# Linear attention and an MLP on one core: the first batch's k and v over all 128 partitions, its products in array quarters

## The chip, the core and the metric

The kernel runs on one core of a Trainium2 chip. Its engines work side by side, each through its own queue in order: TensorE (PE) multiplies matrices into PSUM, VectorE (DVE) and ScalarE (ACT) compute on SBUF and PSUM, GpSimd (POOL) computes and issues DMAs, SyncE (SP) issues DMAs. The metric is the device time of one execution in microseconds; the shown times are the median of several runs.

## The reference

Eight batches of eight heads, 576 tokens, 64 values to a head, float32 in and out. Linear attention, then a layer norm and an MLP with a residual:

```python
q_s = exp(q - max) / sum over d          # softmax of each token's q
k_s = exp(k - max) / sum over tokens     # softmax of each column of k
kv  = einsum('bhsd,bhse->bhde', k_s, v)  # 64 x 64 for each head
x   = einsum('bhsd,bhde->bhse', q_s, kv) # -> [B, S, 512]
xn  = (x - mean) / sqrt(var + 1e-6) * g_ln
out = x + relu(xn @ w_ch1) @ w_ch2       # 512 -> 2048 -> 512
```

## The kernel before, in words

The work is cut into nine chunks: chunk b of 0 to 7 is the first 512 tokens of batch b, four tokens to a partition, and chunk 8 gathers the last 64 tokens of all batches. For each chunk the attention gives x, x is centred, transposed so that the model dimension lies on the partitions (`xnT`), multiplied by w1 (2048 columns, `ph` or `bx`, `bb`, `bc`), passed through relu to `hT`, and multiplied by w2. From chunk 1 on both MLP products go by a scheme of seven block products instead of eight. The whole program has its order written out by hand: `run` (L820), under `tc.manual_schedule` (L1071), interleaves a list of MLP products with side work that has a place in units of PE time. Each engine's queue is the order of these calls.

The change touches the prologue, `first_batch` (L938), which makes the first two of chunk 0's four token groups ready for the MLP:

- SP issues the loads of q's tokens 0 and 1 (L951) and then of k in four pieces of two heads (L961). Batch 0's k and v hold all 576 tokens, six to a partition on 96 partitions (`T0`, `P0`, L56).
- DVE clears and fills constants (L968 to L982), among them `kv_sb[:, 1:B]`, whose off-diagonal blocks must be zero for the later batches.
- POOL makes the identity, then copies four columns of q into `gate` (L985). That copy waits for q's landing, and everything behind it in POOL's queue waits with it: the loads of v in three pieces with a cast to bf16 (L987), of q's tokens 2 and 3 (L951), of w1 (L994, L99) and w2 (L103).
- PE runs products on a tile of zeros (`warm`, L838). ACT takes exp of q (L209), DVE sums and normalises it (L218, L264, L904), PE transposes it (`eq_pT`, L909).
- ACT takes exp of k for two heads at a time (`exp_k0`, L283). PE sums it over the tokens by products with a column of ones (`z0_mm`, L296): six products for each pair of heads. `recip_z` (L304) inverts the sums.
- `kv0_mm` (L311): six products of exp(k) with v for a pair of heads, 96 rows by 128 columns each. Only the two 64x64 diagonal blocks of the result are wanted. DVE multiplies by the reciprocal and by a block-diagonal mask `diag` in one instruction and sums each row (L312). ACT (for the last pair DVE) spreads the row sum, times -1/512, over 128 columns, `mbc` (L317, L321).
- `xT_mm` (L332) multiplies `kv_sb` and `mbc` by the transposed exp(q), which gives x centred and transposed straight away in `pxT`; `xT_out` (L341, L343) scales it by g into `xnT`. In between stand exp and transposes of q's tokens 2 and 3.

Then the MLP of chunk 0 begins (`mm1_part`, L505). Its first 16 products need w1's first 512 columns, which come in two pieces (L994). `kv_pairs` (L361) is the later batches' k'v, in two column halves of the array, and `po_mm` (L395) is chunk 8's x, in all four quarters.

Of the kernel before, what the change touches and what calls it, by code (L numbers as in the profile page):

```python
# [12 lines left out]
FP32 = mybir.dt.float32  # L13
BF16 = mybir.dt.bfloat16
AF = mybir.ActivationFunctionType
ALU = mybir.AluOpType
# [4 lines left out]
def kernel(  # L21
# [16 lines left out]
    nc = tc.nc  # L38

    B, H, S, D = q.shape  # L40
    DM = H * D
    DH = 4 * DM
    P = 128
# [3 lines left out]
    KO1 = DM // P  # L47
    KO2 = DH // P
    NP = H // 2
# [3 lines left out]
    C9 = B  # L53
    FAST = 1
    CAST = (1, 2, 3)
    T0 = 6  # L56
    P0 = S // T0
    assert SR == 64 and B % 2 == 0

    const = ctx.enter_context(tc.tile_pool(name="const", bufs=1))  # L60
    wts = ctx.enter_context(tc.tile_pool(name="wts", bufs=1))
    raw = ctx.enter_context(tc.tile_pool(name="raw", bufs=2))
    att = ctx.enter_context(tc.tile_pool(name="att", bufs=2))
    sml = ctx.enter_context(tc.tile_pool(name="sml", bufs=8))
    mlp = ctx.enter_context(tc.tile_pool(name="mlp", bufs=2))
# [3 lines left out]
    att_ps = ctx.enter_context(tc.tile_pool(name="att_ps", bufs=2, space=PS))  # L69
    mm_ps = ctx.enter_context(tc.tile_pool(name="mm_ps", bufs=6, space=PS))  # L70

    ident = const.tile([P, P], BF16)
    eps_ln = const.tile([P, 1], FP32)
    gate = const.tile([P, 4], FP32)
    ones = const.tile([P, 1], BF16)
    junk = const.tile([P, 256], BF16)
    scrap = const.tile([P, 512], BF16)
    bones = const.tile([P, 2], BF16)
    ones_w = const.tile([P, P], BF16)
    diag = const.tile([P, P], FP32)  # L80
    mbc = const.tile([P, NP, P], BF16)
    g_one = const.tile([P, KO1], FP32)
    w1_sb = wts.tile([P, KO1, DH], BF16, name="w1_raw")
    w1g = const.tile([P, KO1, DH], BF16)
# [1 line left out]
    ident_f = const.tile([KO1, KO1], FP32)  # L86
    w2_sb = const.tile([P, KO2, DM], BF16)
    w2_q = const.tile([P, 4, KH, DH2], BF16)
    kv_sb = const.tile([P, B, NP, P], BF16)
    ekr = const.tile([P, 2, H // 2, D], BF16)  # L90
    vr = const.tile([P, 2, H, VW], BF16)
    vm = const.tile([P, 2, T, H, VW], BF16)

    w1_src = moe_w_ch1.rearrange("(ko ki) n -> ki ko n", ki=P)
    w2_src = moe_w_ch2.rearrange("(ko ki) n -> ki ko n", ki=P)

# [11 lines left out]
    raws = {}  # L108
# [66 lines left out]
    eks, eqs, eqTs, xs, xnTs, rstds, tqs = {}, {}, {}, {}, {}, {}, {}  # L175
# [101 lines left out]
    kvbox = {}  # L277

    def exp_k0(j):
        hs = slice(2 * j, 2 * j + 2)  # L280
        if j == 0:
            eks[0] = raw.tile([P, T0, H, D], BF16, tag="kt", name="ek0", bufs=1)
        nc.scalar.activation(  # L283
            eks[0][0:P0, :, hs, :].rearrange("p t h d -> p h t d"), raws[0][0][0:P0, hs], AF.Exp
        )

    def k0_mm(j, t):
        hs = slice(2 * j, 2 * j + 2)
        return eks[0][0:P0, t, hs, :], raws["v0"][0:P0, hs, t, :], P

    def z0_mm(j):

        if j == 0:
            kvbox["z0"] = mm_ps.tile([P, NP], FP32, tag="m", name="z0")
        for t in range(T0):
            nc.tensor.matmul(  # L296
                kvbox["z0"][:, j : j + 1], k0_mm(j, t)[0], ones[0:P0],
                start=(j == 0 and t == 0), stop=(t == T0 - 1), skip_group_check=True,
            )

    def recip_z():
        kvbox["rz"] = sml.tile([P, NP], FP32, tag="rzk", name="rzk")
        kvbox["sum"] = sml.tile([P, NP], FP32, tag="lnv", name="kvs")
        nc.vector.reciprocal(kvbox["rz"], kvbox["z0"])  # L304

    def kv0_mm(j):
        pool, tag = (att_ps, "a") if j < 2 else (mm_ps, "m")
        pkv = pool.tile([P, P], FP32, tag=tag, name="pkv")
        for t in range(T0):
            lhsT, rhs, w = k0_mm(j, t)  # L310
            nc.tensor.matmul(pkv[:, 0:w], lhsT, rhs, start=(t == 0), stop=(t == T0 - 1))  # L311
        nc.vector.scalar_tensor_tensor(  # L312
            kv_sb[:, 0, j, :], in0=pkv, scalar=kvbox["rz"][:, j : j + 1], in1=diag,
            op0=ALU.mult, op1=ALU.mult, accum_out=kvbox["sum"][:, j : j + 1],
        )
        if j < NP - 1:
            nc.scalar.activation(  # L317
                mbc[:, j], ones_w, AF.Copy, scale=kvbox["sum"][:, j : j + 1]
            )
        else:  # L320
            nc.vector.tensor_scalar_mul(  # L321
                out=mbc[:, j], in0=ones_w, scalar1=kvbox["sum"][:, j : j + 1]
            )

    def xT_mm(j, kh):

        if j == 0:
            pobox["T", kh] = mm_ps.tile([P, 2, 2, P], FP32, tag="m", name="pxT")
        ops = [(kv_sb[:, 0, j, :], j % 2)] if j // 2 == kh else []
        ops += [(mbc[:, j], i) for i in range(2)]  # L330
        for n, (lhsT, i) in enumerate(ops):
            nc.tensor.matmul(  # L332
                pobox["T", kh][:, i], lhsT, eqTs[0][:, 0:2, j, :],
                start=(j == 0 and n == 0), stop=(j == NP - 1 and n >= len(ops) - 2),
                skip_group_check=True,
            )

    def xT_out(i):
# [2 lines left out]
            nc.vector.tensor_scalar_mul(out=dst, in0=src, scalar1=g_one[:, i : i + 1])  # L341
        else:
            nc.scalar.activation(dst, src, AF.Copy, scale=g_one[:, i : i + 1])  # L343

    halves = (slice(0, 64), slice(64, P))

    def kv_pairs(b, ts=range(T + 1)):

# [589 lines left out]
    def first_batch():  # L938

        nc.scalar.preload_act_table_set("natural_log_exp_and_others")  # L940
        raws[0] = (
            mlp.tile([P, H, T0, D], FP32, tag="hT", name="kt0", bufs=1), None,
            raw.tile([P, H, T, D], FP32, tag="qt", name="qt"),
        )
        k0, _, q0 = raws[0]
        v0 = mlp.tile([P, H, T0, D], BF16, tag="hs", name="v0", bufs=1)
        raws["v0"] = v0

        def load_q0(t, tn, eng):
            ts = slice(t, t + tn)  # L950
            eng.dma_start(  # L951
                q0[:, :, ts],
                q[0, :, 0:SM, :].rearrange("h (p t) d -> p h t d", t=T)[:, :, ts],
            )

        def src0(x, h0, hn):
            return x[0, h0 : h0 + hn].rearrange("h (p t) d -> p h (t d)", t=T0)

        load_q0(0, 2, nc.sync)
        for h0 in range(0, H, 2):  # L960
            nc.sync.dma_start(  # L961
                k0[0:P0, h0 : h0 + 2].rearrange("p h t d -> p h (t d)"), src0(k, h0, 2)
            )
        raws["g"] = outp.tile([KO1, P], FP32, tag="ot", name="g_rows")
        nc.scalar.dma_start(
            raws["g"], bass.AP(moe_g_ln.tensor, moe_g_ln.offset, [[P, KO1], [1, P]])
        )
        nc.vector.memset(junk, 0.0)  # L968
        nc.vector.memset(eps_ln, 1e-6)
        nc.vector.memset(ones, 1.0)  # L970
        nc.vector.memset(bones, 0.0)
        nc.vector.memset(bones[0:64, 0:1], 1.0)
        nc.vector.memset(bones[64:P, 1:2], 1.0)
        nc.vector.memset(ones_w, -1.0 / DM)
        nc.vector.memset(diag, 0.0)
        for ps in halves:
            nc.vector.memset(diag[ps, ps], 1.0)
        nc.vector.memset(kv_sb[:, 1:B], 0.0)
        nc.vector.memset(vr, 0.0)
        for half in range(2):  # L980
            nc.vector.memset(vr[64 * half : 64 * half + 64, :, 4 * half : 4 * half + 4, D:], 1.0)
        nc.vector.memset(vm[:, :, :, :, D:], 1.0)  # L982
        make_identity(nc, ident)
        nc.gpsimd.tensor_copy(out=ident_f, in_=ident[0:KO1, 0:KO1])
        nc.gpsimd.tensor_copy(out=gate, in_=q0[:, 1, 0, 0:4])  # L985
        for h0, hn in ((0, 4), (4, 2), (6, 2)):
            nc.gpsimd.dma_start(  # L987
                v0[0:P0, h0 : h0 + hn].rearrange("p h t d -> p h (t d)"), src0(v, h0, hn)
            )
        for t in range(2, T):  # L990
            load_q0(t, 1, nc.gpsimd)
        for kh in range(2):
            ks = slice(2 * kh, 2 * kh + 2)
            nc.gpsimd.dma_start(w1_sb[:, ks, 0:512], w1_src[:, ks, 0:512])  # L994
        for nb in range(1, 4):
            load_w1(nb)
        load_w2(0)
        load_w2(1)

        new_eq(0)  # L1000
        start_x(0)
        warm(34)
        for t in range(2):
            exp_qt(0, t)
            norm_q(0, t)
        eq_pT(0, 0, nc.vector)
        warm(11)
        eq_pT(0, 1, nc.vector)
        for j in range(NP):
            exp_k0(j)  # L1010
            z0_mm(j)
            if j == NP - 2:
                g_columns()
        recip_z()
        kv0_mm(0)
        kv0_mm(1)
        kv0_mm(2)
        xT_mm(0, 0)
        kv0_mm(3)
        exp_qt(0, 2)  # L1020
        exp_qt(0, 3)
        xT_mm(1, 0)
        xT_mm(2, 0)
        xT_mm(0, 1)
        xT_mm(3, 0)
        xT_out(0)
        xT_out(1)
        eq_pT(0, 2, nc.scalar)
        xT_mm(1, 1)
        xT_mm(2, 1)  # L1030
        eq_pT(0, 3, nc.vector)
        xT_mm(3, 1)
        xT_out(2)
        xT_out(3)
# [139 lines left out]
```

## Time and profile before

| | us |
|---|---|
| median of 3 runs (264.06, 264.73, 266.44) | 264.73 |
| span of the profiled execution | 262.95 |
| between the two | 1.8 |
| PE busy, idle in the span | 255.6, 7.3 |
| first MLP product (`ph`) starts | 15.04 |
| w1's second piece landed | 16.89 |

The span runs from the first to the last instruction of one profiled execution; the runs' times are those of whole executions, and the difference is what lies around the span. In lines of the timeline the first number is the start in us, the second how long, then engine, line, operation, output and inputs, count, and in brackets the idle time before and what ended it. Lines of groups give busy us, mean ns of one, and idle time. PEld is the loading of the stationary operand, which overlaps PE.

The granted TensorE clock is 0.998 over the span.

### The profile page before, as it was taken

The page shows a single profiled execution, that of the slowest core. Times are in us where ns is not written, and L with a number is a line of the kernel's source. Part 1 is how long each engine was busy: PE and PEld are TensorE (multiplying, and loading weights), DVE is VectorE, ACT ScalarE, POOL GpSimd, SP SyncE. Part 2 cuts the span into 40 slices and gives each one's busy share as a digit, 9 for nine tenths or more (in the row PEclk, how much of TensorE's full clock was granted, in tenths as well). Part 3 has the DMA queues.
Part 4 walks back from the last instruction along what each step waited for, and adds up shares of the span by engine and source line. Part 5 has one row for each costly group of instructions (what it writes and reads, how often), then busy time and mean ns, then how long its engine had stood idle before and what let it go on. Part 6 is the DMA issues. An engine that isn't in the chain of part 4 may idle for free.

```text
span 262.9 us, 6770 instructions
## 1 busy us (share of the span) xinstructions
PE 255.6 (97%) x2656; PEld 220.1 (84%) x2659; DVE 223.4 (85%) x504; ACT 176.8 (67%) x348; POOL 94.2 (36%) x148
## 2 busy tenths in 40 slices
PE   8999999999999999999999999999999999999993
PEld 6789755788878998899899988988898888888882
DVE  6768996989998999799889988998898979977872
ACT  4647780997976886689578957894789277537400
POOL 4953228414039404930781088009100800030000
PEclk9999999999999999999999999999999999999999
DMA  6999999998999995899489938994905323221014
GB/s 204 252 202 207 358 215 269 282 188 260 187 151 341 232 119 58 266 278 111 100 251 280 140 82 270 261 167 100 271 11 107 113 102 44 42 110 52 0 41 120
DMA packets 82504, 45.00 MB, mean 171 GB/s; under 512 B 58084, under 2 KB 79080, under 8 KB 82472
## 3 DMA queue, kind: packets, MB, share of 16 engines
q0 software_dynamic: 32464, 21.76, 45.3%
q1 hardware_dynamic: 49424, 22.29, 40.1%
q10 hardware_dynamic: 584, 0.53, 0.6%
q8 instruction: 20, 0.33, 0.5%
q14 instruction: 12, 0.10, 0.1%
HBM read 36.70 MB, written 9.44 MB: 175 GB/s over the span
## 4 chain that ended last, share of the span: by engine, by line
PE 89%; DMA 4%; POOL 2%; DVE 2%; issue 1%; ACT 0%; POOLq 0%
PE ba L588 20%; PE bx L733 19%; PE bb L733 10%; PE ph L505 8%; PE be L588 5%; PE bb L588 5%; PE bc L588 5%; PE pc L541 5%; PE bc L733 5%; DMA w_raw<-in_moe_w_ch_dram 3%; PE po L404 2%; PE pkv L361 2%; DMA qt<-in_q_dram 2%; PE ptr L909 1%; POOL v L987 1%; POOL qt L951 1%
## 5 line engine op out<-in xcount | busy, mean ns | idle before, releaser
L588 PEld LDWEIGHTS <-hs 128*128 128x128 bf16 x512 | 49.8, 98 | 5.7
L733 PEld LDWEIGHTS <-w_raw 128*128 128x128 bf16 x480 | 45.5, 98 | 6.4 <-issue 1.2
L259 POOL TENSOR_TENSOR tq<-xnT 128x256 bf16<-128x256 bf16 x26 | 16.7, 662 | 75.3 <-DMA xnT<-xn 48.7
L588 PEld LDWEIGHTS <-hT 128*128 128x128 bf16 x384 | 37.2, 98 | 4.3
L733 PEld LDWEIGHTS <-w1g 128*128 128x128 bf16 x360 | 34.3, 98 | 4.5 <-issue 0.4
L733 PE MATMUL bx<-tq,w_raw 128*128 128x256 bf16 x240 | 31.6, 273 | 0.2 <-ACT s L761 0.2
L588 PE MATMUL ba<-w_q,hs 128*128 128x256 bf16 x256 | 30.8, 273 | 0.0
L757 ACT COPY bc<-bx 128x512 f32<-128x512 f32 x30 | 16.7, 595 | 19.0 <-PE bx L733 19.0
L764 DVE TENSOR_TENSOR bb<-bx,s 128x512 f32<-128x512 f32 x30 | 19.5, 695 | 9.8 <-ACT s L761 7.0
L605 POOL DMA_DIRECT2D out_dram<-ot x28 | 15.4, 557 | 23.7 <-DVE ot L599 23.6
L775 ACT ACTIVATE hT<-bb 128x512 bf16<-128x512 f32 x30 | 16.3, 595 | 10.8 <-PE bb L733 9.6
L417 ACT ACTIVATE scrap<-x,mv 128x512 bf16<-128x512 bf16 x32 | 23.1, 722 | 0.3
L775 ACT ACTIVATE hT<-bc 128x512 bf16<-128x512 f32 x30 | 16.3, 595 | 9.4 <-PE bc L733 9.4
L572 DVE TENSOR_TENSOR hs<-hT 128x1024 bf16<-128x1024 bf16 x32 | 21.7, 685 | 0.5 <-ACT hT L775 0.5
L404 PE MATMUL po<-kv_sb,eqT 128*128 128x128 bf16 x128 | 22.0, 219 | 0.0
L767 DVE TENSOR_TENSOR hT<-bx,s 128x512 bf16<-128x512 f32 x30 | 19.3, 684 | 3.1 <-PE bx L733 3.1
L449 DVE SCALAR_TENSOR_TENSOR x<-po,rq 128x512 bf16<-128x512 f32 x30 | 20.5, 684 | 0.9 <-PE po L404 0.8
L218 DVE TENSOR_REDUCE zq<-eq 128x16 f32<-128x1024 bf16 (+1 forms) x20 | 20.8, 1051 | 0.6 <-ACT eq L209 0.5
L613 ACT COPY s<-ba 128x512 f32<-128x512 f32 x15 | 8.8, 584 | 14.4 <-PE ba L588 9.8
L775 ACT ACTIVATE hT<-bx 128x512 bf16<-128x512 f32 x30 | 16.5, 604 | 0.9 <-PE bx L733 0.9
L761 ACT COPY s<-bb 128x512 f32<-128x512 f32 x30 | 16.6, 622 | 0.6 <-PE bb L733 0.6
L588 PE MATMUL ba<-w_sb,hT 128*128 128x256 bf16 x128 | 16.6, 272 | 0.0
(155 smaller groups left out, 553.5 us busy)
## 6 DMA issues: line engine op xcount, KB each, us to landing
out_dram<-ot POOLq DMA_DIRECT2D x30, 256.0 KB, 5.8
qt<-in_q_dram SPq DMA_DIRECT2D x5, 1024.0 KB, 6.0
kt<-in_k_dram SPq DMA_DIRECT2D x5, 1024.0 KB, 12.5
qt<-in_q_dram POOLq DMA_DIRECT2D x2, 1024.0 KB, 12.9
kt<-in_k_dram POOLq DMA_DIRECT2D x2, 1024.0 KB, 14.3
vm<-in_v_dram POOLq DMA_DIRECT2D x16, 128.0 KB, 11.5
w_raw<-in_moe_w_ch_dram POOLq DMA_DIRECT2D x3, 512.0 KB, 10.9
w_sb<-in_moe_w_ch_dram POOLq DMA_DIRECT2D x3, 512.0 KB, 16.4
```

The source lines that it names most:

```text
L218: nc.vector.reduce_sum(eqs[c][1][:, ts], eqs[c][0][:, ts], axis=AX.X)
L259: eng.tensor_tensor(out=dst[:, t], in0=x[:, t], in1=y[:, t], op=ALU.subtract)
L404: nc.tensor.matmul(pobox["p"][:, i * P : i * P + P], eqTs[c][:, t, i, :], kv_sb[:, c, i, :], start=True, stop=True,)
L417: nc.scalar.activation(scrap, x[:, t], AF.Square, bias=mv[:, t, 0:1], scale=-float(DM), accum_out=mv[:, t, 1:2],)
L449: nc.vector.scalar_tensor_tensor(x[:, t].rearrange("p (h d) -> p h d", h=H), in0=pobox[c, t].rearrange("p (h d) -> p h d", h=H), scalar=1. ...
L505: nc.tensor.matmul(ph[:, m % 2, at : at + tn], (w1g if c else w1_sb)[:, ko, m * P : (m + 1) * P], xnTs[c][:, t0 : t0 + tn, ko, :], start=( ...
L572: nc.vector.tensor_tensor(out=dst, in0=x, in1=y, op=op)
L588: nc.tensor.matmul(hbox[bank][:, t], lhsT, rhs, start=first and (own or t == 0) and k == 0, stop=k == KH - 1, skip_group_check=True)
L733: nc.tensor.matmul(dst[:, q], lhsT, rhs, start=first and q == 0 and ko == 0, stop=ko == 1, skip_group_check=True)
L764: nc.vector.tensor_tensor(out=at[g, "b"], in0=at[g, "x"], in1=at[g, "s"], op=ALU.add)
L767: nc.vector.tensor_tensor(out=h_out(g, 1, 1), in0=at[g, "x"], in1=at[g, "s"], op=ALU.add)
L775: nc.scalar.activation(h_out(g, odd, half), at[g, name], AF.Relu)
```

## The change

Batch 0's k and v lie nine tokens to a partition, 64 partitions to a head, two heads above each other on the 128 partitions. A pair of heads is one piece, contiguous in HBM: k comes in four DMAs of 128 x 576 as before on SP, v in three on POOL. Each of `z0_mm` and `kv0_mm` now makes nine products for the upper and nine for the lower head, alternating, on rows and columns 0 to 63 and 64 to 127 of the array: 72 products of 64x64 for each of the two steps, where there were 24 of 96x128. Their results lie in two PSUM tiles each. The reciprocal becomes two of 64 partitions. Of k'v, DVE scales and sums the upper block and ACT the lower one; the mask goes, and batch 0's `kv_sb` is cleared ahead. The mean column is one value to a partition (`kvm`, on DVE), and PE reads it 128 times with step 0.

On POOL the copy into `gate` goes, and the clearing of `kv_sb[:, 1:B]`, 3584 bf16 on each partition, comes from DVE to POOL, ahead of the loads of v. On DVE two constants go (`ones_w`, `diag`), and `ones_f` and `kv_sb[:, 0]` come.

```diff
-    T0 = 6
-    P0 = S // T0
+    T0 = 9
...
     def z0_mm(j):
         if j == 0:
-            kvbox["z0"] = mm_ps.tile([P, NP], FP32, tag="m", name="z0")
+            kvbox["z0"] = [mm_ps.tile([P, NP], FP32, tag="m", name="z0") for _ in halves]
         for t in range(T0):
-            nc.tensor.matmul(
-                kvbox["z0"][:, j : j + 1], k0_mm(j, t)[0], ones[0:P0],
-                start=(j == 0 and t == 0), stop=(t == T0 - 1), skip_group_check=True,
-            )
+            for z0, ps in zip(kvbox["z0"], halves):
+                nc.tensor.matmul(
+                    z0[ps, j : j + 1], eks[0][ps, j, t], ones[ps],
+                    start=(j == 0 and t == 0), stop=(t == T0 - 1), skip_group_check=True,
+                )
...
     def kv0_mm(j):
-        pool, tag = (att_ps, "a") if j < 2 else (mm_ps, "m")
-        pkv = pool.tile([P, P], FP32, tag=tag, name="pkv")
+        pkv = [
+            pool.tile([P, D], FP32, tag=tag, name="pkv")
+            for pool, tag in ((att_ps, "a"), (mm_ps, "m"))
+        ]
         for t in range(T0):
-            lhsT, rhs, w = k0_mm(j, t)
-            nc.tensor.matmul(pkv[:, 0:w], lhsT, rhs, start=(t == 0), stop=(t == T0 - 1))
+            for pk, ps in zip(pkv, halves):
+                nc.tensor.matmul(
+                    pk[ps], eks[0][ps, j, t], raws["v0"][ps, j, t],
+                    start=(t == 0), stop=(t == T0 - 1),
+                )
...
         nc.vector.scalar_tensor_tensor(
-            kv_sb[:, 0, j, :], in0=pkv, scalar=kvbox["rz"][:, j : j + 1], in1=diag,
-            op0=ALU.mult, op1=ALU.mult, accum_out=kvbox["sum"][:, j : j + 1],
-        )
-        if j < NP - 1:
-            nc.scalar.activation(
-                mbc[:, j], ones_w, AF.Copy, scale=kvbox["sum"][:, j : j + 1]
-            )
-        else:
-            nc.vector.tensor_scalar_mul(
-                out=mbc[:, j], in0=ones_w, scalar1=kvbox["sum"][:, j : j + 1]
-            )
+            kv_sb[lo, 0, j, lo], in0=pkv[0][lo], scalar=rz[lo], in1=ones_f[lo],
+            op0=ALU.mult, op1=ALU.mult, accum_out=total[lo],
+        )
+        nc.scalar.activation(
+            kv_sb[hi, 0, j, hi], pkv[1][hi], AF.Copy, scale=rz[hi], accum_out=total[hi]
+        )
+        nc.vector.tensor_scalar_mul(out=kvm[:, j : j + 1], in0=total, scalar1=-1.0 / DM)
...
-        ops += [(mbc[:, j], i) for i in range(2)]
+        ops += [(kvm[:, j : j + 1].to_broadcast([P, P]), i) for i in range(2)]
...
-        nc.vector.memset(kv_sb[:, 1:B], 0.0)
+        nc.vector.memset(ones_f, 1.0)
+        nc.vector.memset(kv_sb[:, 0], 0.0)
+        make_identity(nc, ident)
+        nc.gpsimd.tensor_copy(out=ident_f, in_=ident[0:KO1, 0:KO1])
+        nc.gpsimd.memset(kv_sb[:, 1:B], 0.0)
+        for j0, jn in ((0, 2), (2, 1), (3, 1)):
+            nc.gpsimd.dma_start(
+                v0[:, j0 : j0 + jn].rearrange("p j t d -> p j (t d)"), src0(v, j0, jn)
+            )
...
-        nc.gpsimd.tensor_copy(out=gate, in_=q0[:, 1, 0, 0:4])
-        for h0, hn in ((0, 4), (4, 2), (6, 2)):
-            nc.gpsimd.dma_start(
-                v0[0:P0, h0 : h0 + hn].rearrange("p h t d -> p h (t d)"), src0(v, h0, hn)
-            )
```

## The prediction

> **What bounds the kernel now.** I read the page first, then the chain of waits of the first 30 us, then the timeline of the first 20 us, and last the rows nearest to what the change adds.
>
> ```profile
> PE 255.6 (97%) x2656; PEld 220.1 (84%) x2659; DVE 223.4 (85%) x504; ACT 176.8 (67%) x348; POOL 94.2 (36%) x148
> ...
> DMA  6999999998999995899489938994905323221014
> ```
>
> TensorE is busy for 255.6 of 262.9 us. Everything that the change touches lies in the first 17 us, so it can only pay by letting PE reach its unbroken stretch sooner. The DMA digits say that the 16 DMA engines are full from the first slice on.
>
> ```profile
> 0.74 4.03 DMA qt<-in_q_dram
> ...
> 4.82 0.19 POOL gate L985
> 5.00 2.06 POOL v L987 x3
> 7.07 1.84 POOL qt L951 x2
> 8.91 0.64 POOL w_raw L994
> 9.56 7.33 DMA w_raw<-in_moe_w_ch_dram
> ```
>
> The chain runs q, gate, POOL's DMA issues, then 7.33 us until the second piece of w1 lands at 16.89; there PE goes on. It looks as if the gate cost time. It does not by itself. The windows of this stretch show a DMA share of 1.10 to 1.29 in each 2 us from 4 us on (over 1 means two packets in flight), and the trace's packet records show the first v packet at 7.68, 2.7 us after its issue, just when SP's k packets run out (last at 7.93). The same is seen later: stores that POOL issued at 81.66 send nothing before 85.30, when SP's loads of 77.5 to 80.4 run out. So w1 waits for bytes, not for its issue at 9.56.
>
> ```profile
> 8.71 0.40 PE L909 MATMUL ptr<-ident,eq 128*128 128x128 bf16 x4
> 8.95 0.59 PE L296 MATMUL z<-ones,ek 96*128 96x1 bf16 x18
> 9.47 0.38 PE L934 MATMUL gcp<-ident_f,g_rows 4*128 4x4 f32 x2
> 10.32 1.25 PE L311 MATMUL pkv<-v,ek 96*128 96x128 bf16 x18 [0.24 <-DMA v<-in_v_dram]
> 11.71 0.39 PE L332 MATMUL pxT<-eqT,mbc 128*128 128x256 bf16 x2
> 13.39 0.39 PE L332 MATMUL pxT<-eqT,mbc 128*128 128x256 bf16 x2 [0.19 <-DVE mbc L321]
> 15.03 0.33 PEld L505 LDWEIGHTS <-w_raw 128*128 128x128 bf16 x4 [0.21 <-DMA w_raw<-in_moe_w_ch_dram]
> 16.93 0.33 PEld L505 LDWEIGHTS <-w_raw 128*128 128x128 bf16 x4 [0.38 <-DMA w_raw<-in_moe_w_ch_dram]
> ```
>
> This is PE's own path: transposes of exp(q) at 8.71 (they follow q, ACT and DVE, which the change leaves alone), denominators, k'v, x transposed, and the first MLP products at 15.03. At 16.93 w1 is 0.38 us late. So two paths end almost together: PE's own, with 0.38 us to spare, and DMA's.
>
> **The change part by part.**
>
> POOL: the gate goes, but a memset of 3584 bf16 on each partition stands in its place ahead of the v loads.
>
> ```profile
> masks.py:197 POOL MEMSET ident<- 128x128 bf16 x1 | 0.2, 204 | 0.3 <-POOLq L1158 0.3
> L1158 POOL MEMSET const-bfloat16-1.0<- 128x1 bf16 x1 | 0.1, 102 | 0.0
> ```
>
> 127 more elements take 102 ns, 0.80 ns each, so the memset takes 0.10 + 3583 x 0.80 = 3.0 us. It follows the cast that ends at 1.55, so v is issued at about 4.6 against 4.94. The bounds are nothing (v at 1.6) and 2.6 ns an element, POOL's slowest row here (662 ns for 256 in L259), 9.3 us. I take 3.0, since it is the same operation. v's packets can't start before k's are through at about 7.6, so 0.3 us earlier gains nothing; a memset up to about 4.9 us would also cost nothing (a POOL DMA with SP idle sent its first packet 1.1 us after issue, 208.09 to 209.22).
>
> DMA: k and v each go from 768 packets to 512 larger ones. The records show 80 ns for v's packet (1536 B read) and 100 ns for w1's (2048 B read), so 2304 B take about 111: 512 x 111 / 16 = 3.55 us instead of 3.84. k: 28.6 ns for 512 B, 80.6 for 1536, so about 120 ns, 3.83 instead of 3.87. Together 0.3 us, w1's second piece at about 16.6. Bounds: nothing, and 80 ns whatever the size, which would free 2.5 us.
>
> DVE loses 1.55 us of memset at 2.4 to 4.0 and some small ones. Its first real work starts at 5.46, just after ACT's first exp(q) ends at 5.42, so this gains nothing. ACT's four exp(k) shrink from 768 to 576 elements (about 0.65 instead of 0.84 each) and end near 8.9, held by k's landing; PE reaches the last of them later than that. Nothing again.
>
> PE: 24 denominator products become 72, and 24 k'v products become 72, in alternating quarters. The nearest rows are the later batches' k'v in two column halves, and batch 8's products in all four quarters:
>
> ```profile
> 42.07 0.32 PE L361 MATMUL pkv<-vm,ek 128*64 128x65 bf16 x8
> 42.70 0.20 PE L361 MATMUL pkv<-vr,ekr 128*64 128x65 bf16 x2
> ```
> ```profile
> 210.40 0.45 PE L395 MATMUL po<-kv_sb,eqT 64*64 64x64 bf16 x32
> 210.78 0.77 PEld L733 LDWEIGHTS <-w_raw 128*128 128x128 bf16 x8
> ```
>
> 40 products start within 0.64 us: 16 ns each, two tiles side by side. 32 start within 0.45 - 0.19: 8 ns each, four tiles. The new code alternates two tiles, so I take 16 ns. Entering such a mode costs about 0.1 us and so does leaving it (PE was due at 210.31 and started at 210.40; it left at 210.66 and went on at 210.78). The new order switches six times: into z, out and in around the g column product, out at the first x product, in and out around the fourth k'v.
>
> The path then is: z starts at 9.05 (8.95 + 0.1); 54 x 16 ns to 9.92; g products at 10.0; the last 18 from 10.43 (0.31 as now, 0.1 for the switch) to 10.72. k'v follows at once, since v's first part lands at about 10.1: the first ends at 11.2 (10.83 now). The four take 1.15 us instead of 24 x 59 ns = 1.4.
>
> Evictions: two reciprocals (0.18 each) end at 11.25. DVE's half takes about 0.30 (351 ns for 128 elements, 686 for 512); ACT's about 0.38 (469 ns for 256 and 592 for 512) and 0.2 for its accumulator; the mean column, a 128x1 op like L467, 0.14. From 11.26 this ends at 12.04, and the first x product on it starts there, at 11.71 now. DVE's queue is in order, so the next half waits behind the mean column, which waits for ACT; a round takes 0.5 to 0.6 us. k'v 2 also waits for the first att_ps buffer (DVE, 11.56), and k'v 3 for the second (about 12.33). The last mean column is ready near 13.7, where mbc was at 13.34. ACT's last half ends near 13.5, so its exp(q) of token 2, 12.55 to 13.18 now, ends at about 14.15, and the transposes behind it on PE wait 0.2 us. The first MLP product comes at about 15.5 instead of 15.03, the second w1 piece is reached at 16.55 + 0.49 = 17.04, where it has landed.
>
> The mean column read with step 0 has no row. Bounds: nothing (the 16 loads of mbc take 97 ns and hide under 107 ns steps), and about 1 us, if a load without the wide path takes as long per column as the 64-column ones (110 ns, so 220) and half of that hides. I take nothing: the count of columns is the same.
>
> Sum: PE's path is 0.49 later, 0.38 of it was waiting anyway: +0.11 us on the execution's span, 263.05. The span shown is 262.95; 264.73 - 262.95 = 1.8 us lie around it by the median, so **264.8 us**.
>
> **The rivals.**
>
> A, slower: the two quarters do not overlap, and each product costs what a product of today costs, 25 ns for z (18 within 0.59 - 0.16) and 59 for k'v. 48 more of each are 1.2 + 2.8 us, less the 0.3 that I counted (2.30 for all against 2.0 now): +3.7 on the forecast, 268.5. It decides from an average step of 34 ns on ((2.6 us / 144) + 16). The 8 and 16 ns rows speak against it; that none of them alternates just two quarters on the diagonal speaks for it.
>
> B: the quarters overlap, but no product starts less than 25 ns after the one before, today's z step: 144 x 9 ns = 1.3 us, 266.1. Against it stand the 8 and 16 ns rows. The Trainium skill, "TensorE: Matmul & The Clock Gate", section "Wait — 56ns, not 53.3ns?", states this floor, about 25 ns however small the product; by it the time would be 266.1, and the traced 8 and 16 ns disagree.
>
> C: v's packets take turns with k's as soon as they exist, at about 5.7 (4.6 + 1.1). k, with 2.2 us to go, would end up to 2.2 us later, at 10.1; the last exp(k) ends at 10.8 and the last z at 11.1, 0.4 after mine: 265.2. For it: the gate's place. Against it: the stores of 81.66 that did not start beside SP's loads. The Trainium skill, "DMA: Bandwidth & Descriptors", section "Queues, rings and completion order", has each engine go round its queues packet by packet, which speaks against ungating v; by that the time is 265.2, and the 3.6 us wait at 81.66 disagrees.
>
> D, a little faster: the quarters run at 8 ns, 144 x 8 = 1.2 us sooner. Then w1's landing at 16.6 decides: 264.73 - 0.3 = 264.4. More is not to be had, whatever POOL and DVE save.
>
> E, slower: the memset takes 2.6 ns an element. v is issued at 10.9 and sends from 12.0; today 9.2 us pass from v's first packet (7.68) to w1's second landing (16.89), so that comes at about 20.9, 4.0 us late: 268.7. It decides from 2.1 ns an element on (1.37, where it begins to cost, and 2.65 us more over 3583).
>
> **How the numbers follow.** Forecast 0.52, D 0.17, B 0.12, C 0.07, A 0.08, E 0.04. The runs before spread from 264.06 to 266.44. The low end is D less that spread's lower part (0.6), 263.8; the high end is B with 0.5 for a partly slow step-0 load, 266.6. A and E are left out (0.12). One per cent, 2.65 us, is about what a measurement of this kernel can tell from no change. Slower by more: A and E, 0.12. Faster by more: no case gives it, 0.02 for what I did not see. Within 1%: 0.86.
>
> **What would show it.** POOL's memset at 1.6 for 3.0 us, v issued near 4.6, its first packet still near 7.6; 18 z products within 0.3 us; first MLP product at 15.3 to 15.7, no w1 wait at the second piece. Wrong if that piece is reached after 17.5 or before 16.6, if the step-0 loads are longer than 97 ns, or if a wait appears after 20 us that is not there now.

## The result, and the profile after

The kernel after takes 265.38 us (median of 22 runs, 264.28 to 266.80), the kernel before on the same chip 264.31 (22 runs, 263.27 to 267.87): a ratio of 1.0039, with a 95% interval of 1.0022 to 1.0056. It is about 1.0 us slower, within 1% of before.

The profiled execution of after has a span of 263.41 us and a time of 265.19. Two lines of its page, the busy sums and the granted clock in 40 slices:

```profile
PE 257.5 (98%) x2755; PEld 221.6 (84%) x2755; DVE 221.9 (84%) x505; ACT 176.4 (67%) x353; POOL 97.1 (37%) x148
...
PEclk9979999999999999999999999999999999999998
```

PE has 96 products more to do and is busy 1.9 us longer. The third digit of the clock is new: one slice, early, has less than the full clock. The windows of that stretch, cut close to the ends of the clock's own records (columns: window, length, busy us and count of PE, PEld, DVE, ACT and POOL, granted clock, DMA share, GB/s):

```profile
5.80:9.20 3.40, 3.38 (x36) 2.54 (x36) 3.15 (x7) 2.63 (x5) 3.40 (x6) 1.00 1.04 246
9.20:12.60 3.40, 3.20 (x140) 2.89 (x141) 1.99 (x13) 1.09 (x6) 2.99 (x5) 1.00 1.04 231
12.60:16.00 3.40, 3.40 (x35) 2.60 (x32) 1.44 (x6) 2.08 (x5) 2.19 (x3) 0.50 1.16 178
16.00:19.40 3.40, 3.34 (x44) 2.87 (x43) 1.85 (x8) 1.42 (x4) 1.65 (x2) 1.00 1.24 207
```

From 12.60 to 16.01 the clock is halved. The window before it holds the quarter products, and PE counts as busy for 3.20 of its 3.40 us. The same stretch of before, with PE busy for less of it, keeps the whole clock, as does the stretch behind it:

```profile
9.20:12.60 3.40, 3.14 (x52) 2.67 (x50) 1.97 (x11) 1.46 (x5) 3.40 (x6) 1.00 1.21 270
12.60:16.00 3.40, 3.21 (x38) 2.54 (x36) 2.21 (x7) 2.63 (x5) 2.78 (x4) 1.00 1.21 193
```

The chain of waits of the first 30 us no longer runs through DMA:

```profile
9.20 0.94 PE z L288 x54
...
11.63 0.47 PE pkv L307 x18
12.10 0.43 PE pxT L329 x3
12.53 0.55 PE pkv L307 x18
13.08 2.04 PE pxT L329 x9
15.12 0.43 PE ptr L904 x4
15.54 0.84 PE pxT L329 x5
```

Where before's chain ended in w1's landing (7.33 us of it), PE's own path is now last. The timeline of PE shows the same products:

```profile
9.13 1.01 PE L288 MATMUL z<-ones,ek 64*64 64x1 bf16 x54
...
10.39 0.44 PE L288 MATMUL z<-ones,ek 64*64 64x1 bf16 x18
10.69 0.73 PE L307 MATMUL pkv<-v,ek 64*64 64x64 bf16 x36
...
12.15 0.38 PE L329 MATMUL pxT<-eqT,kvm 128*128 128x256 bf16 x2
...
13.20 1.92 PE L329 MATMUL pxT<-eqT,kvm 128*128 128x256 bf16 x8
14.91 0.63 PE L904 MATMUL ptr<-ident,eq 128*128 128x128 bf16 x4
...
16.77 0.60 PE L500 MATMUL ph<-xnT,w_raw 128*128 128x256 bf16 x4
```

Eight x products take 1.92 us, 213 ns apart. Six of the same products in before's timeline are 107 ns apart:

```profile
12.39 0.81 PE L332 MATMUL pxT<-eqT,mbc 128*128 128x256 bf16 x6
```

The first MLP product starts at 16.77 instead of 15.04, 1.73 us late. Yet the span is only 0.46 us longer. The waits of PE in before tell why:

```profile
PE bb L733 <- POOL tq L259: 0.6, 1, 0.6
```

Before's profiled execution lost about 1.1 us around 78 us (this wait and what followed it, L733 behind POOL and ACT); after's did not. From `ba`'s first product to its last, 192.42 us pass in after, e1, e6, e8, e9 and e10 alike, and 193.5 in before. So the start of the MLP is what counts in these kernels, and one execution's span is off by up to 1.1 us for other reasons. The verdicts below rest on medians; the profiles say where.

The spans of the single runs bear this out: the median is 263.6 us in the 22 runs of after and 261.9 in the 101 runs of before that stand beside the experiments. That is 1.7 us, as much as the start of the MLP lost. The times of the result are only about 1.0 apart, for two reasons. The 22 runs of before beside after have a median 0.4 us above that of the 101 (263.89). And between span and time lie 1.8 us in every run of after, but 1.7 to 3.1, on average 2.05, in the 101 of before. In e10 below, which keeps the old layout, it is 1.8 in every run as well, so this does not go with the layout; what it is, no run shows.

### The profile page after: what moved, and what is told of

The parts are those of the page before. It is cut to its first block, busy times and chain, and to the rows that moved or that the text cites. A ratio compares the mean times of both kernels' runs of the same rounds, so it can differ in the third digit from the quotient of the medians.

```text
span 263.4 us, 6976 instructions
## 1 busy us (share of the span) xinstructions
PE 257.5 (98%) x2755; PEld 221.6 (84%) x2755; DVE 221.9 (84%) x505; ACT 176.4 (67%) x353; POOL 97.1 (37%) x148
## 4 chain that ended last, share of the span: by engine, by line
PE 95%; DVE 3%; issue 0%; DVEq 0%
PE ba L583 21%; PE bx L728 20%; PE bb L728 10%; PE ph L500 8%; PE bc L583 5%; PE be L583 5%; PE bb L583 5%; PE pc L536 5%; PE bc L728 5%; PE warm L833 3%; PE po L399 2%; PE pkv L356 2%; PE ptr L904 2%; PE pxT L329 1%; DVE kv_sb L364 1%; DVE x L444 1%
## 5 line engine op out<-in xcount | busy, mean ns | idle before, releaser
L752 ACT COPY bc<-bx 128x512 f32<-128x512 f32 x30 | 16.6, 594 | 19.0 <-PE bx L728 19.0
L583 PE MATMUL ba<-w_sb,hT 128*128 128x256 bf16 x128 | 16.6, 273 | 0.0
L756 ACT COPY s<-bb 128x512 f32<-128x512 f32 x30 | 16.6, 622 | 0.0
## 6 DMA issues: line engine op xcount, KB each, us to landing
kt<-in_k_dram POOLq DMA_DIRECT2D x2, 1024.0 KB, 14.6
```

The lines of the kernel that those rows point to most:

```text
L583: nc.tensor.matmul(hbox[bank][:, t], lhsT, rhs, start=first and (own or t == 0) and k == 0, stop=k == KH - 1, skip_group_check=True)
```

## The experiments

Twelve kernels, in five rounds each against the kernel before. "Old layout" is six tokens to a partition, "new" is nine. The third column is the ratio to before with its 95% interval; then come, from each profiled execution, when the last x product and the first MLP product start, when w1's first piece landed, and whether a halved clock falls into the prologue of that one execution.

| kernel | median, us | ratio | last x | first MLP | w1 landed | halved |
|---|---|---|---|---|---|---|
| before | 264.31 | 1 | 14.83 | 15.04 | 14.99 | no |
| e1, old: gate and memset only | 263.84 | 1.0008 (0.9985 to 1.0031) | 14.42 | 15.82 | 15.78 | no |
| e8, old: step 0, addresses kept | 264.09 | 1.0001 (0.9973 to 1.0029) | 14.45 | 16.57 | 16.52 | no |
| e10, old: more rows of PE's program | 264.20 | 1.0005 (0.9985 to 1.0025) | 15.78 | 15.91 | 15.86 | no |
| e2, old: step 0, addresses moved | 266.08 | 1.0085 (1.0057 to 1.0113) | 16.18 | 16.29 | 15.93 | no |
| e7, old: addresses moved alone | 266.30 | 1.0084 (1.0056 to 1.0113) | 15.59 | 15.70 | 15.29 | no |
| after, new | 265.38 | 1.0039 (1.0022 to 1.0056) | 16.66 | 16.77 | 15.66 | yes |
| e3, new, gate and `mbc` as before | 265.51 | 1.0059 (1.0037 to 1.0082) | 17.99 | 18.09 | 16.28 | yes |
| e4, new, 8 products fill | 265.45 | 1.0061 (1.0033 to 1.0088) | 16.88 | 16.99 | 15.67 | no |
| e5, new, shorter warm-up | 264.87 | 1.0034 (1.0011 to 1.0058) | 15.97 | 16.08 | 15.74 | no |
| e6, new, both | 264.87 | 1.0037 (1.0014 to 1.0060) | 16.33 | 16.44 | 15.50 | no |
| e9, e5 with v in halves | 265.14 | 1.0029 (1.0005 to 1.0052) | 16.41 | 16.52 | 16.42 | yes |
| e11, e9 with DVE for the last pair | 265.29 | 1.0052 (1.0033 to 1.0072) | 15.09 | 16.24 | 16.20 | no |
| e12, e11 with 4 products fill | 265.02 | 1.0027 (1.0000 to 1.0055) | 17.19 | 17.30 | 15.60 | yes |

Medians of before were 263.83 with e1 to e4, 264.00 with e5 to e8, 264.03 with e9 and e10, 263.96 with e11 and e12.

**The parts alone.** My first theory was the halved clock.

e1, in the kernel before:

```diff
-        nc.vector.memset(kv_sb[:, 1:B], 0.0)
...
-        nc.gpsimd.tensor_copy(out=gate, in_=q0[:, 1, 0, 0:4])
+        nc.gpsimd.memset(kv_sb[:, 1:B], 0.0)
```

e2, in the kernel before (the evictions that made `mbc` give way to `kvm` as in after, 156 ns on DVE):

```diff
-    mbc = const.tile([P, NP, P], BF16)
+    kvm = const.tile([P, NP], BF16)
...
-        ops += [(mbc[:, j], i) for i in range(2)]
+        ops += [(kvm[:, j : j + 1].to_broadcast([P, P]), i) for i in range(2)]
```

e3 is after with `gate`, DVE's clearing of `kv_sb` and `mbc` put back as they were. e4, in after, with products of 128x128 on 256 columns of zeros into a tile that nothing reads:

```diff
             if j == NP - 2:
+                fill(4)
                 g_columns()
...
         kv0_mm(1)
+        fill(4)
         kv0_mm(2)
```

> The kernel before with one part alone: the copy that waits for q is replaced on POOL by the clearing of kv_sb, which leaves DVE. Theory 1 (the quarter products use so little of the array that its clock is halved for one window of 3.4 us): this part has nothing to do with it; clock near 0.998, v issued near 4.5, first MLP product at 15.0, w1's second piece near 16.9, ratio 0.998 to 1.002. Rival (the load order moved and made the start later): w1 later than 17.2 and ratio above 1.003.

> The kernel before with one part alone: the mean column is one value to a partition, made on DVE and read by PE with step 0. Theory 1: no loss; the 16 step-0 loads take 97 to 100 ns as those of mbc, the clock stays whole, the wait of 0.47 us for the last mbc shrinks to about 0.2, first MLP product 14.8 to 15.0, ratio 0.998 to 1.001. Rival (a step-0 load is slow in itself, which the 134 ns mean in the changed kernel could mean): loads over 120 ns at full clock, first MLP product after 15.5, ratio above 1.003.

> The changed kernel with gate, DVE's clearing and the spread mean column mbc put back: the nine-token layout and the quarter products alone. Theory 1: the halved clock stays (a record of 0.5 for 3.4 us that begins between 11 and 14), x products start every 213 ns in it, first MLP product at 16.5 to 17.2, ratio 1.003 to 1.006, all of the loss. Rival (the loss comes from the two-engine eviction and the in-order mean column): with mbc back the first MLP product comes at 15.5 or sooner, ratio below 1.002.

> The changed kernel with eight junk products of 128x128x256 on the zero tile: four after the third group of z products, four ahead of the third k'v; they add nothing to the output. They cost 8 x 0.107 = 0.86 us of PE, some 0.2 of it in a wait that is there anyway. Theory 1: they keep the array's use high enough, no record of 0.5 between 9 and 17, x products every 107 ns, first MLP product at 15.9 to 16.2 instead of 16.77 although PE has more to do; ratio 0.2 to 0.4 per cent below the changed kernel's 1.0039. Rival (the clock does not depend on this, the path is long by its evictions): first MLP product at 17.3 or later, ratio 1.005 to 1.007.

e1: the gate and the memset together are worth nothing that these runs can tell. e3: the new layout carries the loss without them and without the step-0 read; in its profile the MLP starts at 18.09, later than expected (16.5 to 17.2), with a wait of 1.3 us of k'v for v. e2 was a surprise, taken up below. e4 kept the clock whole in its profile and gained nothing, where 0.2 to 0.4% were expected, so the halved clock alone is not the price. The timeline of PE in e4:

```profile
14.60 0.40 PE L904 MATMUL ptr<-ident,eq 128*128 128x128 bf16 x4
15.88 0.39 PE L329 MATMUL pxT<-eqT,kvm 128*128 128x256 bf16 x2 [0.89 <-issue]
```

The queue of instructions among e4's DMAs from 13.5 to 14.6 us (packets, MB, time as a share of 16 engines' 1.1 us):

```profile
q8 instruction: 1, 0.02, 5.1%
```

PE stands for 0.89 us ahead of a product that waits for no semaphore. It is row 444 of PE's program (a row is one load or one product, in the order of the trace); a packet of 16384 B of instructions was under way from 13.60 to 14.49. It had ended 0.5 us before PE stood still, and 1.4 us before PE went on. That it held PE's next rows, and that PE waited for them, is inferred and not shown. The new layout brings 192 rows more ahead of the first MLP product (452 instead of 260).

**PE's program and the clock.** The second theory: either the halved clock or the wait for PE's program is enough to hold the MLP.

In `warm`, for e5 in after and for e6 in e4:

```diff
-        for _ in range(n):
-            nc.tensor.matmul(w[:, 0:width], junk[:, 0:P], junk[:, 0:width], start=True, stop=True)
+        twice = junk.rearrange("p (o n) -> p o n", o=1).to_broadcast([P, 2, 256])
+        for _ in range(n // 2):
+            nc.tensor.matmul(
+                w.rearrange("p (o n) -> p o n", o=2), junk[:, 0:P], twice, start=True, stop=True
+            )
...
```

e10, in the kernel before:

```diff
-        warm(34)
+        for n in range(120):
+            ps = slice(64 * (n % 2), 64 * (n % 2) + 64)
+            nc.tensor.matmul(w[ps, 0:1], junk[ps, 0:64], junk[ps, 0:1], start=True, stop=True)
+        warm(18)
```

> The kernel after, but the 45 junk products of the warm-up become 23 (22 of them 512 columns wide instead of 256), for the same busy time: PE executes 44 instructions fewer before it gets to the x products. Theory 2, made after e4: PE's program comes to it in packets of 16384 B (256 instructions); the quarter products bring 192 instructions more ahead of the first MLP product (452 against 260), so that PE reaches the end of what it holds before the next packet is there. In e4 it stood from 15.00 to 15.88 waiting for nothing else, with the packet taking 13.60 to 14.49. This kernel should have no such wait, but the granted clock can still be 0.5 for one stretch of 3.4 us: then first MLP product 16.5 to 16.9 and about 265.3 us, as after; in an execution where the clock stays whole, 15.4 to 15.8. Theory 1 (the clock alone) expects the same 265.3. Rival (q's tokens 2 and 3 land late, and everything behind them): 265.4 whatever PE's program and clock do.

> e4 (8 junk products over the whole array among the quarters, which held the clock) together with the shorter warm-up of e5 (44 instructions of PE fewer). Theory 2 with theory 1 (either the halved clock or the wait for PE's program is enough to hold the first MLP product until 16.8 to 17.0; only both away help): clock 1.0 throughout, no stand of PE without a cause at 15.0, first MLP product 15.4 to 16.0 instead of 16.99, and 264.2 us, about 1 us under e4. Theory 1 alone: as e4, 265.4. Rival (late q): as e4, 265.4, with the transposes of q's tokens 2 and 3 waiting for ACT and ACT for DMA.

> The kernel before with 120 junk products of 64x64 on one column put in place of the first 16 junk products of its warm-up: about the same PE time at a moment where PE has nothing to do, but 208 rows more of PE's program ahead of the first MLP product (row 468 instead of 260). Nothing else is changed. Theory 2 (PE's program arrives in packets, and the first one after the start lands too late if PE uses its rows up faster): PE stands without a cause at the same row 444 as in e4, here the x product behind the transposes of q's third token, from about 13.6 until some 1.4 us after the end of the instruction packet, about 16.5; first MLP product 17.0 to 17.4 instead of 15.04, and 265.3 to 266.0 us. Rival (the stand in e4 was something else): first MLP product 15.0 to 16.0 and 263.6 to 264.3 us.

e5 and e6: no such stand in their profiles, and 264.87 each, 0.5 to 0.6 us under after and e4; their ratios overlap with those, so the step is likely, not certain. Neither came back to 264.2, which the second theory had expected of e6.

The clock of the single runs says more. A mean clock under 0.995 means a halved stretch somewhere in the execution (at the end in a few, which the mean can't tell apart). In after, 16 runs under 0.995 take 265.50 us on average and 6 runs over it 265.38: a whole clock gains nothing. In e5, e6, e9, e11 and e12, which have 44 rows of PE's program fewer (e6 and e12 28 and 36), 22 runs under 0.995 take 265.55 and 35 runs over it 264.88, 0.67 less (e11 alone shows no difference). So in after the clock is masked, and in the kernels with a shorter program it counts. That the length of the program decides this is not shown: e4 has the longest of the new layout, and there 2 runs under 0.995 take 266.15, 6 over it 265.42. In e1, of the old layout, 2 runs under it take 265.43 and 10 over it 263.81, a whole 1.6 us. These are associations over runs, not edits.

What the layout does to the clock is clear from all runs: under 0.995 are 48 of the 96 of the new layout and 8 of the 157 of the old one. Which execution it hits is in part chance. The clock's records are multiples of 3.41 us long and begin elsewhere in each execution. The window ahead of the halved one begins at 9.19 in after, 9.94 in e3, 8.85 in e9 and 8.58 in e12, so that it takes in most of the quarter products; e5 and e11, which have no fill, have a boundary at 10.71, amid these products, and the clock stays whole. One profile with a whole clock therefore does not show that an edit kept it whole. For the fill speak the runs: under 0.995 are 2 of 8 in e4 and 16 of 22 in after, but 3 of 12 in e6 and 5 of 12 in e5, which is no clear difference.

e10 missed. It has 208 rows more and no stand: its instruction packet came at 6.37, not at 14.42, so more rows early also fetch early. My expectation had left that out. The stand at row 444 was thus seen in one profile only. e10 did show what such a packet costs: it took 1.22 us of one DMA engine, and the third piece of k landed at 9.41 (8.32 in e8).

**The addresses.** e2 differed from before in more than its step-0 read: `kvm` takes 32 B on each partition where `mbc` took 1024, so all later buffers moved by 992 B, to 32 past a multiple of 64.

e7, in the kernel before:

```diff
     mbc = const.tile([P, NP, P], BF16)
+    pad = const.tile([P, 8], FP32)
```

e8, in e2:

```diff
-    kvm = const.tile([P, NP], BF16)
+    kvw = const.tile([P, NP, P], BF16)
+    kvm = kvw[:, 0, 0:NP]
```

> The kernel before with an unused tile of 32 B per partition behind the broadcast mean columns, so that every later tile starts 32 B higher: k's, v's, q's and w1's buffers start 32 B past a multiple of 64 instead of on one. Nothing else is changed. Theory A (in e2 it was the address that slowed k's packets from 80.6 to 103.9 ns, since dropping the 1024 B broadcast columns for 32 B moved every later buffer to 32 past a multiple of 64): k's packets 100 to 105 ns, last one near 9.3, first MLP product near 16.2, 265.8 to 266.1 us. Theory B (it was the step-0 read, or chance): 263.8, k's packets near 81 ns.

> e2 (the kernel before with the mean column read with step 0) with the mean columns inside a tile as large as the broadcast columns were, so that all later buffers keep the addresses of before. Theory A (addresses): k's packets back near 81 ns and 263.4 to 264.0 us, the step-0 read costing nothing. Theory B (the step-0 read costs): 265.8 to 266.1, as e2.

Theory A holds in the main: an unused tile of 32 B costs 0.84%, and the step-0 read with the addresses kept costs nothing that these runs can tell. Groups of e8, the loads and products of the step-0 operand:

```profile
L328 PE MATMUL pxT<-eqT,kvw 128*128 128x256 bf16 x16 | 2.6, 274 | 0.0
...
L328 PEld LDWEIGHTS <-kvw 128*128 128x128 bf16 x16 | 1.4, 98 | 0.3 <-DVE kvw L317 0.2
```

98 ns for a load and 274 for a product, as `mbc` took (97 and 274). In after the same load takes 134 ns on average, which is the halved clock: in e5, whose clock is whole, it takes 98. Less of e7's loss lies in the prologue than expected: its MLP starts at 15.70, not near 16.2, and from there to the end of the span pass 248.8 us, where e1 and e8 take 246.8 and 246.7. Two of its waits of PE show most of that:

```profile
PE bb L734 <- POOL tq L260: 1.0, 1, 1.0
PE pkv L362 <- ACT ekr L188: 0.5, 1, 0.5
```

After itself is not touched by this: `kvm` and the other new tiles together moved its buffers to multiples of 512.

**What is left.** With the clock whole and the program short, about 0.8 us remain. The DMA issues of before at 4.4 to 9.7 us (count, KB each, median us from issue to landing):

```profile
qt<-in_q_dram POOLq DMA_DIRECT2D x2, 256.0 KB, 5.4
w_raw<-in_moe_w_ch_dram POOLq DMA_DIRECT2D x2, 256.0 KB, 6.7
...
v<-in_v_dram POOLq DMA_DIRECT2D x2, 144.0 KB, 5.3
```

The same of after:

```profile
qt<-in_q_dram POOLq DMA_DIRECT2D x2, 256.0 KB, 6.8
w_raw<-in_moe_w_ch_dram POOLq DMA_DIRECT2D x2, 256.0 KB, 7.7
...
v<-in_v_dram POOLq DMA_DIRECT2D x2, 144.0 KB, 6.1
```

And of e9, told of below:

```profile
v<-in_v_dram POOLq DMA_DIRECT2D x4, 144.0 KB, 3.9
qt<-in_q_dram POOLq DMA_DIRECT2D x2, 256.0 KB, 4.3
w_raw<-in_moe_w_ch_dram POOLq DMA_DIRECT2D x2, 256.0 KB, 7.9
```

In after, q and w1 take 1.4 and 1.0 us longer to land than in before, with issues 0.6 us sooner. The packet records of after show single packets of v of up to 1009 ns where most take 107, and of q of up to 785 where before has at most 195. Before has such packets too, but few: one of v's took 800 ns, one of w1's 824. Taking, from 4 to 15 us, all packet time beyond 1.6 times the median of the packet's size, and a sixteenth of it for 16 engines: 0.00 to 0.19 us in the six kernels of the old layout, 0.65 to 0.89 in all eight of the new one.

e9, in e5:

```diff
-        for j0, jn in ((0, 2), (2, 1), (3, 1)):
-            nc.gpsimd.dma_start(
-                v0[:, j0 : j0 + jn].rearrange("p j t d -> p j (t d)"), src0(v, j0, jn)
-            )
+        for j0, jn in ((0, 2), (2, 2)):
+            for ps in halves:
+                nc.gpsimd.dma_start(
+                    v0[ps, j0 : j0 + jn].rearrange("p j t d -> p j (t d)"), src0(v, j0, jn)[ps]
+                )
```

e11, in e9, and e12, which adds to e11 two junk products ahead of `kv0_mm(2)` and two behind it:

```diff
+        if j < NP - 1:
             nc.scalar.activation(
                 kv_sb[hi, 0, j, hi], pkv[1][hi], AF.Copy, scale=rz[hi], accum_out=total[hi]
             )
+        else:
+            nc.vector.scalar_tensor_tensor(
+                kv_sb[hi, 0, j, hi], in0=pkv[1][hi], scalar=rz[hi], in1=ones_f[hi],
+                op0=ALU.mult, op1=ALU.mult, accum_out=total[hi],
+            )
```

> e5 (after with the shorter warm-up) with v's three loads (128 partitions each) replaced by four of 64 partitions each, so that its packets are dealt out to the DMA engines in another pattern. Theory 3: what is left of the loss in e5 and e6 (0.9 us with the clock whole and no wait for PE's program) comes from single packets that take 260 to 1050 ns instead of 106: 12 to 20 of v's and some of q's and w1's in every kernel with the nine-token layout (30 to 59 in all before 20 us), at most 7 in before, e1 and e8. They put the first k'v product at 11.44 (a wait of 0.75 for v) and q's last packet at 13.4 to 13.8 instead of 12.4 to 12.7. If the pattern of v's load makes them, they go here: v's packets 106 to 110 ns, last one before 11.0, first MLP product 15.0 to 15.6, 263.6 to 264.2 us. If it is the packets' size or k's layout, they stay: 30 or more long packets and 264.7 to 265.2 us, as e5. Rival (the last ACT half of k'v ahead of exp(q) is what is left): long packets or not, 264.7 to 265.2.

> e9 (after with the shorter warm-up and v loaded in four halves) with both halves of the last k'v product scaled on DVE, so that ACT's exp of q's third and fourth token no longer stands behind ACT's half of that product (in e9 that exp began at 13.41 though its token had landed at 11.32). Theory 4, made from e1 to e10: the first MLP product starts when two things are both there, w1's first piece (landed 15.0 to 16.5 in the profiles of the old layout, 15.5 to 16.4 in those of the new one, so alike) and the x products. In the old layout the x products are done by 14.5 to 15.7 and w1 decides; in the new one they end at 15.9 to 16.9, held by the halved clock, or by PE's program, or by late q, or by this exp, whichever is last. Expected where the clock stays whole: x products done by 15.2, first MLP product with w1's landing, 15.3 to 16.4, and a median of 263.9 to 264.4 us, as before. Rival (the new layout costs its 0.9 us elsewhere, such as in the long packets of w1): 264.8 to 265.3, as e9.

> e11 with 4 junk products over the whole array put where PE waits in e9 (2 ahead of the third k'v product, 2 behind it), to hold the clock. Theory 4: no execution with a clock under 0.992 (e9 had 3 of 12), x products done by 15.4, first MLP product with w1's landing, 263.9 to 264.4 us, at most 0.2 from e11. Theory 1 in its first form (the halved clock is the price): clearly under e11 if that still shows halved clocks. Rival (the loss is elsewhere): 264.8 to 265.3.

e9 moved the long packets instead of removing them: v's last packet came at 10.18 (11.67 in after) and q's at 11.75 (13.67), but w1's packets took their place (0.76 us by the measure above), and w1's first piece landed at 16.42. e11 did to PE's path what was meant, as its timeline shows:

```profile
14.98 0.38 PE L335 MATMUL pxT<-eqT,kvm 128*128 128x256 bf16 x2
16.24 0.61 PE L506 MATMUL ph<-xnT,w_raw 128*128 128x256 bf16 x4 [0.88 <-DMA w_raw<-in_moe_w_ch_dram]
```

The x products are done 1.6 us sooner than in after, and the MLP waits for w1, landed at 16.20. The time did not move: 265.29. Theory 4 expected 263.9 to 264.4 and fell; its rival, that the new layout costs its share elsewhere, in w1's long packets, gave 264.8 to 265.3. e12, at 265.02, falls to the rival as well, and its profile shows that 4 products can be too few to hold the clock: it is halved from 11.99 to 15.40.

**Verdict.** Shown: the gate, the memset and the step-0 read cost nothing that can be told (intervals of 0.2 to 0.3% to either side); the new layout costs 0.3 to 0.6% in every form tried (the interval of e12 begins at 1.0000); x products ready at 15.1 do not bring it back. Argued from sizes that fit, and not shown, since no edit removed the long packets: about 0.8 us by the long packets, and the rest by the halved clock, or by PE's program where the clock is whole. The sizes: runs with a clock over 0.995 take 264.88 in the five kernels above, and 263.81, 264.22 and 264.31 in e1, e8 and e10, 264.11 on average; the measure of the long packets is 0.65 to 0.89. By the spans of the same runs, 263.1 and 262.1 on average, the gap is 1.0 us, and the fit is looser. Open: why the new layout's packets stall. It has packets of 2304 B read instead of 1536, on 128 partitions instead of 96; no run told these apart. No version beat the kernel before.

## Why the prediction was right or wrong

It forecast 264.8 us (263.8 to 266.6) with "within 1%" at 0.86. The time, 265.38, is in the range, and it is within 1%. The sum said +0.11 us; the runs say +1.0. So the range and the class were right and the mechanism was not: by the prediction's own signs it was wrong, since w1's second piece was reached at 18.29, later than 17.5, and the step-0 loads were longer than 97 ns. That the number still came out close is in part luck. The base of 264.73 came from three runs; 22 runs give 264.31, on which the same sum would have said 264.4. And the start of the MLP came 1.3 us later than forecast, of which the time shows less than the span.

- POOL: memset 3.0 us forecast, 3.08 measured; v's issue "about 4.6", 4.53. The groups of after: 

```profile
L974 POOL MEMSET kv_sb<- 128x3584 bf16 x1 | 3.1, 3075 | 0.0
```

  Rival E is out.
- "v's packets can't start before k's are through": k's last packet starts at 7.34, v's first at 6.78, so engines that are done with k go on to v and do not take turns. e1, with v issued at 4.52, has v's first packet at 7.66, k's last at 8.17. That v gains nothing without the gate is right, and rival C is out: k is through at 7.44, not at that rival's 10.1. The Trainium skill, "DMA: Bandwidth & Descriptors", section "Queues, rings and completion order", would have had them take turns; this trace disagrees.
- DMA, the first mis-sized term: k's packets took 93 ns, not 120 (2.98 us instead of 3.83, a gain), but v's 120.6 on average with 107 for most (3.86 instead of 3.55), and q's 215 instead of 185. w1's second piece landed at 16.99, where "about 16.6" was forecast. I had priced packets by size alone, one after the other, and had left out single long ones, of which before already has a few (0.18 us by the measure above).
- PE's quarters: 16 ns a product was right (54 within 1.01 - 0.19 us), z started at 9.13 (9.05), the last 18 at 10.39 (10.43), the first x product on the mean column at 12.15 (12.04), the last mean column was ready at 13.74 ("near 13.7"). Rivals A, B and D are out; the floor of 25 ns of B does not hold for these products.
- "The first MLP product comes at about 15.5": the step that failed. Up to 13.7 the path ran as worked out; then the x products came 107 ns further apart, 1.3 us for the twelve between 13.02 and 16.0, and 15.5 became 16.77. I had taken the clock of before, whole from 5.93 us on, for granted, though I replaced full products by quarters in the stretch just ahead. That the layout brings the halved clock is shown by the runs (48 of 96 against 8 of 157); what about the quarters does it is not. The halved stretch is 3.41 us long. The Trainium skill, "TensorE: Matmul & The Clock Gate", section "What's actually happening", has such a window of about 3.4 us running freely, and half the clock after an idle one; the length agrees, but here the window before was 94% busy by the profile (3.20 of 3.40), so busy time in the profile's sense is not what it goes by.
- "To be reached at 17.04, where w1 has landed": at 18.29, and it had. The reserve of 0.38 us that I set against the delay was thus used up more than once.
- The step-0 read "nothing": right (e8, 1.0001); the 134 ns of its loads in after are the clock's. What I did not ask is where the smaller tile puts everything behind it; after was lucky there, e2 was not.
- The execution of before that I summed against lost 1.1 us around 78 us, which most of the others do not. Its span of 262.95 is 1.1 us over the median of before's runs, 261.9, so as a base it was no typical one.

## What to carry to other kernels

When small products on part of the array replace full ones, count the rows of PE's program and look at the granted clock of the next 3.4 us, not only at product times; a stretch can be "busy" and still lose the clock, in some executions and not in others. Before removing or shrinking a tile, look at the addresses of every tile behind it, since 32 B can cost more than the edit saves. And where PE and a load end almost together, shortening one of them shows nothing until the other is shortened as well.

## What the runs showed of the hardware that was not expected

- Buffers that start 32 B past a multiple of 64: q's packets of 4096 B took 251 and 254 ns (e7, e2) instead of 185, k's of 1536 B 97 and 104 instead of 81 to 88 (before, e1, e8); v's, which are cast on the way, stayed at 79. The whole kernel lost 2.3 us. The Trainium skill, "DMA: Bandwidth & Descriptors", section "How a descriptor splits into AXI transactions", says that a descriptor that does not start on 256 B takes an extra transaction; for 4096 B that would be an estimated 17 instead of 16 at most, 6%, and the trace shows 36%.
- An instruction packet of 16384 B holds up one DMA engine for 0.89 to 1.22 us, and every transfer waits for its slowest engine. In e1, 15 of the 16 engines had finished w1's first piece by 14.19 us, the last at 15.78, with an instruction packet from 13.74 to 14.69.
- A halved stretch of 3.41 us could cost 1.7 us at most. Runs with a mean clock under 0.995 took 1.6 us more in e1 (2 runs), 0.67 in the kernels with the shorter program, 0.1 in after: the less, it seems, the more else is late.
- The clock's windows of 3.41 us begin at another time in each execution, so the same kernel has runs with and without a halved stretch.
